# W_out products in merged runs, the last store in halves, and one 40-column product in the attention stage

## The chip, the cores and the metric

The kernel runs on one core of a Trainium2 chip. Its engines are TensorE (PE, with its weight loads shown apart as PEld), VectorE (DVE), ScalarE (ACT), GpSimd (POOL) and SyncE (SP, which here only issues DMAs). The metric is the device time of one launch in microseconds (us); lower is better.

## The reference

Three stages follow one another: a two-step attention over packed tokens, a mixture of experts with one expert for each token, and a dense layer pair with a sigmoid gate. Cut to what matters:

```
p_packed = sm_attn(p, k, v)                    # 8 batches, 8 heads, 576 tokens of 64; 32 packed tokens
x        = sm_attn(q, p_packed, p_packed)      # softmax attention, then tokens x 512
logits   = normed(x) @ normed(expert_emb).T / tau     # 8 experts
out[t]   = gate[t] * (relu(x[t] @ w1[e]) @ w2[e]),  e = argmax(logits[t])
h        = out @ w_in                          # 4608 x 512 by 512 x 2048
y        = (h * sigmoid(h)) @ w_out            # 2048 x 512
```

## The kernel before, in words

**Attention (`attention`, lines 1497 to 1890).** For each of 8 batches, `keys` makes the scores of the packed queries, `packs` the packed values and `queries` the second attention. Every operation is recorded with a cost, and `Sched.run` then makes one order for all engines: it takes the operation that can start first by these costs, with the table `TIMES` as priority. A changed cost or a changed buffer therefore moves work all over this stage. SP's loads keep the order in which they are recorded.

`packs` runs two times per batch (t = 0, 1). It transposes the packed values into PSUM, copies them to a tile `ppT` (a ring of two), and from `ppT` come three things: two POOL copies into `pt2` (line 1703), one POOL copy into `R.pp` (1709), and a small PE group `mp`: four products of 32 columns (values by values, line 1716) and four of 8 columns (values by expert embeddings `enT`, line 1719). DVE then takes `mp` into `ppf` (lines 1724, 1725), the operand of `queries`.

**Experts (from about 180 us) and the first dense layer (`group`, to about 850 us).** The change leaves both as they are. All matrix products are in split precision: an operand is a rounded high part (`hi`, a cast on ACT) and the rest (`lo`, a subtraction on DVE). The first dense layer writes its results as 2x2 blocks c11, c12, c21, c22 of a seven-product (Strassen-like) scheme into the DRAM tiles `c_d`.

**W_out (the end of `ffn`, from about 850 us).** There are 18 units `u` (each 256 rows of the output); a unit is seven products, in the order 1, 7, 6, 2, 5, 3, 4 (`order3`). Product i takes an operand of 128x1024: 1 and 6 take c11, 7 takes c21, 2 takes c12, 5 takes E1, 3 takes S4, 4 takes c22. `split(s)` makes its `hi` (ACT, line 1169) and `lo` (DVE) into one of four slots, two products ahead of use; the slots repeat with s mod 4. Besides, DVE makes the sums c11 = E1 - c11, S4 = c12 - c11 and, for the 14 units from u = 4 on, c21 = c11 - c21. For those units E1 is made by two DMAs into one tile: a plain load issued by SP (line 1186) and an adding one issued by POOL (line 1187) once the first has landed; the next unit's pair is started by `early_sums` when this unit's E1 has been split. `load_unit` loads the four blocks of the unit after the next.

From u = 2 on a product is "wide": eight matmuls of 512 columns with `hi` as weights (against high and low part of the output weights side by side, line 1202), then eight of 256 columns with `lo` (line 1200). Only the last unit's product 4 is narrow (256 columns throughout, lines 1204, 1205). A unit has four PSUM banks, and the units take two sets in turn: 1 and 2 add up in the first bank, 6 and 5 in the second, 7 and 4 in the third, 3 in the fourth. `drain` takes a bank into SBUF between them: P1 (after 1), U2 (after 6), V (after 5), and the two output tiles `outs[u]`; `write` stores these through SP (lines 1246, 1250). A bank's next product waits for the drain.

Of the kernel before, what the change touches and what calls it, by code (L numbers as in the profile page):

```python
# [871 lines left out]
def ffn(tc, st, sums, y_d, wf_d, t_d, c_d, u_d, out):  # L872
# [290 lines left out]
    def split(s):  # L1163
# [16 lines left out]
    def early_sums(u):  # L1180
# [3 lines left out]
        c11, c12, c21, c22 = raws[u % 2]  # L1184
# [3 lines left out]
        tt(DVE, c21, c11, c21, ALU.subtract)  # L1188

    def product(s, gs, start=True, stop=True):  # L1190
# [6 lines left out]
        for g, part in [(g, y) for y in (0, 1) for g in gs]:  # L1197
# [12 lines left out]
    def drain(s):  # L1210
# [16 lines left out]
        elif i == 6:  # L1227
            plus(U2, b, P1)
        elif i == 2:
            alone(outs[u][0][:, 0:256], a)  # L1230
        elif i == 5:
            plus(V, b, P1)
            plus(outs[u][1][:, 256:512], c, V)
# [3 lines left out]
        if i == 5 and not wide(u, 4):  # L1237
            plus(U2, c[1:], U2)
# [4 lines left out]
    def write(z, r, x, o):  # L1243
# [193 lines left out]
    for s in range(len(seq)):  # L1437
# [23 lines left out]
        if s == 4:  # L1461
            make(*more[4])

# [9 lines left out]
def attention(tc, sc, st, early, mid, R, first, ident, q, k, v, p, emb, tau, a2_d, scale, pairs):  # L1473
# [73 lines left out]
    enT = Part(1, [64, H, E])  # L1547

    def setup():
# [29 lines left out]
        op("DVE", 130, lambda: DVE.tensor_copy(out=enT.ap, in_=ep.ap), r=[ep], w=[enT])  # L1579
# [75 lines left out]
    def packs(b):  # L1655
        x2 = pt2[b % NB]
        for t in range(2):
# [39 lines left out]
            tT = T([128, 128], "ppT", 2)  # L1697
            op("PE", 109, lambda a=a, d=d: PE.transpose(out=a.ap, in_=d.ap.rearrange("p i d -> p (i d)"), identity=ident), r=[d], w=[a], hold=[tT])
            op("DVE", dve_c(128), lambda a=a, tT=tT: DVE.tensor_copy(out=tT.ap, in_=a.ap), r=[a], w=[tT])

            def f(tT=tT, t=t):
                for i in range(2):
                    POOL.tensor_copy(out=x2.ap[64 * i:64 * i + 64, 4 * t:4 * t + 4, 32 * i:32 * i + 32], in_=tT.ap[64 * i:64 * i + 64, :].rearrange("p (h j) -> p h j", h=4))
# [3 lines left out]
            def f(tT=tT, t=t):  # L1707
                h = slice(64 * t, 64 * t + 64)
                POOL.tensor_copy(out=R.pp[b][h, :, 32 * t:32 * t + 32], in_=tT.ap[h, :].rearrange("p (c j) -> p c j", c=4))
# [238 lines left out]
```

## Time and profile before

| | us |
|---|---|
| runs shown, median (lowest to highest) of 3 | 1216.39 (1213.45 to 1219.03) |
| the profiled execution's own time | 1214.78 |
| its span on the core | 1212.9 |
| PE busy | 1173.9 (97% of the span) |
| DVE busy | 876.9 (72%) |
| ACT busy | 526.4 (43%) |
| POOL busy | 146.9 (12%) |

Rows are read from this one profiled execution. A busy PE means that some matmul is in flight; since matmuls overlap, the distance from one start to the next, not the duration, is what a matmul costs. Times of day in the rows count from the span's start.

### The profile page before, as it was taken

How to read it: one execution, taken by the hardware profiler on the slowest of the kernel's cores; microseconds unless marked ns; L12 is line 12 of the kernel's file. 1: busy time of each engine (PE TensorE's matmuls, PEld its weight loads, DVE VectorE, ACT ScalarE, POOL GpSimd, SP SyncE). 2: the span in 40 equal slices, each digit the busy share in tenths (PEclk: the TensorE clock that was granted, in tenths of full speed). 3: DMA queues.
4: the chain of work that ended last, by engine and by line, in shares of the span. 5: the costliest groups of instructions: out<-in, count | busy, mean ns of one | idle time of the engine just before them, and what ended most of it. 6: DMA issues, size and time to landing. Idle time of an engine off the chain costs nothing.

```text
span 1212.9 us, 24417 instructions
## 1 busy us (share of the span) xinstructions
PE 1173.9 (97%) x9548; PEld 1034.1 (85%) x9549; DVE 876.9 (72%) x1560; ACT 526.4 (43%) x911; POOL 146.9 (12%) x259
## 2 busy tenths in 40 slices
PE   8788899999999999999999999999999999999998
PEld 7676679999989998978878878889998888888887
DVE  5475877886897883586765585634878888888886
ACT  4565652333343233464445354434643333333342
POOL 3222220221132432100000000002000000000000
PEclk9999999999999999999999999999999999999999
DMA  9979657569668965576876745788855657575652
GB/s 260 258 222 264 213 184 248 189 245 336 248 233 297 341 209 164 168 231 194 312 253 200 233 142 147 229 260 259 273 212 173 189 176 216 161 221 164 208 145 49
DMA packets 228313, 264.62 MB, mean 218 GB/s; under 512 B 32024, under 2 KB 181784, under 8 KB 227680
## 3 DMA queue, kind: packets, MB, share of 16 engines
q1 hardware_dynamic: 213192, 230.66, 59.2%
q0 software_dynamic: 8048, 27.53, 8.4%
q10 hardware_dynamic: 6952, 4.80, 1.3%
q8 instruction: 77, 1.26, 0.4%
q14 instruction: 44, 0.36, 0.1%
HBM read 175.26 MB, written 87.69 MB: 217 GB/s over the span
## 4 chain that ended last, share of the span: by engine, by line
PE 56%; DVE 3%; issue 1%; ACT 1%; DMA 0%; SPq 0%; DVEq 0%; ACTq 0%
PE p L1202 17%; PE p L1200 10%; PE p L906 8%; PE p L908 8%; PE p L907 8%; PE ps L620 2%; DVE x L899 1%; PE p L1205 1%; PE p L1204 1%; PE ps L541 1%; DVE raw L899 0%; DMA raw<-y_d 0%; DVE mh L899 0%; DMA c_d<-x 0%; DVE y L899 0%
## 5 line engine op out<-in xcount | busy, mean ns | idle before, releaser
L899 DVE TENSOR_TENSOR x<-p,x 128x512 f32<-128x512 f32 (+1 forms) x148 | 90.2, 619 | 58.8 <-PE p L908 52.8
L940 ACT ACTIVATE x<-x 128x512 f32<-128x512 f32 (+1 forms) x111 | 66.7, 603 | 137.5 <-DVE x L899 125.5
L620 PE MATMUL ps<-hkm,w2s 128*128 128x288 f32 x768 | 123.5, 296 | 0.0
L620 PEld LDWEIGHTS ps<-hkm,w2s 128*128 128x128 f32 x768 | 108.5, 188 | 5.9 <-DVE cu L678 1.7
L541 PE MATMUL ps<-at,mh 128*128 128x288 f32 x672 | 93.1, 297 | 4.2 <-PEq L735 2.1
L541 PEld LDWEIGHTS ps<-at,mh 128*128 128x128 f32 x672 | 90.5, 188 | 5.4 <-issue 3.5
L1202 PE MATMUL p<-x,x 128*128 128x512 f32 x332 | 90.4, 394 | 0.0
L620 PE MATMUL ps<-hvm,w2s 128*128 128x288 f32 x448 | 85.3, 295 | 0.0
L1202 PEld LDWEIGHTS p<-x,x 128*128 128x128 f32 x332 | 62.7, 189 | 10.8
L620 PEld LDWEIGHTS ps<-hvm,w2s 128*128 128x128 f32 x448 | 68.3, 188 | 0.1
L899 DVE TENSOR_TENSOR x<-p,y 128x512 f32<-128x512 f32 (+1 forms) x57 | 33.1, 581 | 42.8 <-PE p L908 39.1
L899 DVE TENSOR_TENSOR y<-p,y 128x256 f32<-128x256 f32 (+1 forms) x71 | 34.5, 485 | 35.4 <-PE p L1200 27.3
L1169 ACT CAST x<-rawe 128x1024 fp32r<-128x1024 f32 x35 | 36.4, 1051 | 49.5 <-DVE rawe L899 49.5
L620 PE MATMUL ps<-hqm,w2s 128*128 128x288 f32 x320 | 52.7, 294 | 0.0
L544 ACT ACTIVATE hkm<-ps 128x576 fp32r<-128x576 f32 x42 | 27.3, 652 | 55.7 <-PE ps L541 50.0
L630 ACT COPY yb<-ps 128x576 f32<-128x576 f32 x20 | 12.8, 642 | 88.3 <-PE ps L620 84.8
L1202 PE MATMUL p<-t,x 128*128 128x512 f32 x166 | 51.1, 389 | 0.0
L1187 POOL DMA_DIRECT2D x<-c_d x14 | 12.1, 865 | 319.8 <-DMA x<-c_d 223.1
L620 PEld LDWEIGHTS ps<-hqm,w2s 128*128 128x128 f32 x320 | 46.0, 188 | 0.0
L906 PE MATMUL p<-x,t 128*128 128x512 f32 x112 | 43.9, 392 | 1.5 <-DVE x L899 1.0
L591 DVE TENSOR_TENSOR w2s<-w2c,w2s 128x1024 fp32r<-128x1024 f32 x32 | 40.1, 1252 | 7.2 <-ACT w2s L588 7.2
L1222 ACT COPY raw<-p 128x256 f32<-128x256 f32 x18 | 6.7, 373 | 86.4 <-PE p L1200 86.4
(442 smaller groups left out, 3235.1 us busy)
## 6 DMA issues: line engine op xcount, KB each, us to landing
c_d<-x SPq DMA_DIRECT2D x136, 256.0 KB, 2.9
raww1c<-c_d SPq DMA_DIRECT2D x36, 512.0 KB, 6.1
rawe<-c_d SPq DMA_DIRECT2D x36, 512.0 KB, 5.0
w1c<-in_moe_w_dram SPq DMA_DIRECT2D x32, 512.0 KB, 10.4
w2c<-in_moe_w_dram SPq DMA_DIRECT2D x32, 512.0 KB, 4.0
y_d<-yb SPq DMA_DIRECT2D x36, 288.0 KB, 2.1
raw<-y_d SPq DMA_DIRECT2D x36, 256.0 KB, 4.8
x<-c_d SPq DMA_DIRECT2D x18, 512.0 KB, 3.9
```

Of the source, the lines that this page charges most:

```text
L541: PE.matmul(out=a[:, i, 0:H2], lhsT=mh[x][:, t, f], rhs=at[y][:, t, n], start=t == x == y == 0, stop=t == x == 1, skip_group_check=True)
L544: self.nc.scalar.activation(out=self.hT(0, m).rearrange("p (i n) -> p i n", i=2), in_=a[:, :, 0:S // 2], func=ACTF.Relu)
L591: DVE.tensor_tensor(out=l, in0=w2c[c % 2], in1=h.bitcast(F32), op=ALU.subtract)
L620: PE.matmul(out=a[:, i, 0:H2], lhsT=w[:, k, :], rhs=hT(z, k, n), start=w is h and k == z == 0, stop=w is l and k == 7, skip_group_check=True)
L899: eng.tensor_tensor(out=o, in0=x, in1=y, op=op)
L906: PE.matmul(out=o, lhsT=h, rhs=a[0][k][:, 0:n], start=start and k == 0, stop=False, skip_group_check=True)
L907: PE.matmul(out=o, lhsT=h, rhs=a[1][k][:, 0:n], start=False, stop=False, skip_group_check=True)
L908: PE.matmul(out=o, lhsT=l, rhs=a[0][k][:, 0:n], start=False, stop=k == 1, skip_group_check=True)
L940: ACT.activation(out=y, in_=x, func=ACTF.Silu)
L1169: ACT.copy(out=slots[s % R][0], in_=src)
L1200: PE.matmul(out=o, lhsT=l[:, g], rhs=x[:, 0:256], start=False, stop=stop and g == gs[-1], skip_group_check=True)
L1202: PE.matmul(out=bank, lhsT=h[:, g], rhs=x, start=first and g == gs[0], stop=False, skip_group_check=True)
```

## The change

In `ffn`, for u of 2 and more, a unit's products are emitted in three runs: (1, 7, 6), (2, 5) and (3, 4). A run first does the 512-column parts of its products one after another, then their 256-column parts. The drains, the splits and the loads are placed by hand between the 256-column parts. The sums S4 (16 units) and c21 (14 units) go from DVE to POOL. Product 7 is drained early, by an ACT copy and one DVE sum, and V is added later; DVE's count of 256-column drain operations in a unit stays 12. In the last unit the second output tile is stored in two column halves, the first when product 5 is drained, the second after product 4, one of its two DMAs on ACT's queue.

In `attention`, the embeddings stand beside the transposed values in one tile of 40 columns per head pair (`ppT`, now four fixed tiles), so that each group `mp` is four products of 40 columns.

```diff
-                tt(DVE, S4, c12, c11, ALU.subtract)
+                tt(POOL if u > 1 else DVE, S4, c12, c11, ALU.subtract)
...
+    def early_sums(u, loads=True):
+        if loads:
+            early_load(u)
+        if units[u][0] not in FIVE:
+            c11, c12, c21, c22 = raws[u % 2]
+            tt(DVE if loads else POOL, c21, c11, c21, ALU.subtract)
...
-        for g, part in [(g, y) for y in (0, 1) for g in gs]:
+        for g, part in [(g, y) for y in parts for g in gs]:
...
+        elif i == 7 and u > 1:
+            alone(outs[u][1][:, 256:512], c)
...
+                tt(DVE, outs[u][1][:, 256:512], outs[u][1][:, 256:512], V)
+                if u + 1 == len(units):
+                    write(z, r, 1, outs[u][1], slice(256, 512))
...
-            write(z, r, 1, outs[u][1])
+            write(z, r, 1, outs[u][1], slice(0, 256 if u + 1 == len(units) else 512))
...
-                SP.dma_start(out=out[(j + i) * S + 512:(j + i + 1) * S, :], in_=o[64 * i:64 * i + 64, :])
+                (ACT if i and n.stop == 256 else SP).dma_start(out=out[(j + i) * S + 512:(j + i + 1) * S, n], in_=o[64 * i:64 * i + 64, n])
...
+    for u in range(2, len(units)):
+        s = M + (u - 2) * len(order3)
+        for first, run in ((0, 3), (3, 2), (5, 2)):
+            for x in range(first, first + run):
+                product(s + x, range(G), parts=(0,))
+            for x in range(first, first + run):
+                i = order3[x]
+                product(s + x, range(G), parts=(1,))
+                if i not in (1, 7, 3):
+                    drain(s + x)
+                if i == 1:
+                    drain(s)
+                    hi(s + 4)
+                    lo(s + 4)
+                    if u + 1 < len(units):
+                        early_load(u + 1)
+                        early_sums(u + 1, False)
+                elif i == 6:
+                    drain(s + 1)
+                    hi(s + 5)
+                    lo(s + 3)
+                    lo(s + 5)
+                elif i == 2:
+                    hi(s + 6)
+                elif i == 5:
+                    hi(s + 7)
+                    lo(s + 6)
+                    if u + 2 < len(units):
+                        load_unit(u + 2)
+                    lo(s + 7)
+                    hi(s + 8)
+                elif i == 3:
+                    lo(s + 8)
+                    hi(s + 9)
+                    drain(s + x)
+                elif i == 4:
+                    lo(s + 9)
+                    hi(s + 10)
...
-            tT = T([128, 128], "ppT", 2)
+            tT = ppT[b % 2][t]
...
                 for c in range(4):
-                    h = slice(32 * c, 32 * c + 32)
-                    PE.matmul(out=m.ap[h, 0:32], lhsT=tT.ap[0:64, h], rhs=tT.ap[0:64, h], start=True, stop=True)
-                for c in range(4):
-                    h = slice(32 * c, 32 * c + 32)
-                    PE.matmul(out=m.ap[h, 32:32 + E], lhsT=tT.ap[0:64, h], rhs=enT.ap[:, 2 * c + t, :], start=True, stop=True)
-            op("PE", 200, f, r=[tT, enT], w=[m], after=o.users).mode = 3
+                    PE.matmul(out=m.ap[32 * c:32 * c + 32, :], lhsT=tT.ap[0:64, c, 0:NP], rhs=tT.ap[0:64, c, :], start=True, stop=True)
+            op("PE", 130, f, r=[tT], w=[m], after=o.users).mode = 3
```

**Attention, PE.** The order differs from the first `mp` groups of batch 0 on. Before (pptp: transposed packed values; mp: the small group; ktp, krp: transposed keys; s2p, s1p: scores):

```order
L1698 MATMUL pptp<-ident,ppd 128x128
L1716 MATMUL mp<-ppT 32x32 x4
L1719 MATMUL mp<-e_148,ppT 32x8 x4
L1716 MATMUL mp<-ppT 32x32 x4
L1719 MATMUL mp<-e_148,ppT 32x8 x4
L1624 MATMUL ktp<-ident,km 128x128 x8
L1611 MATMUL krp<-ident,kr 128x64 x4
L1753 MATMUL s2p<-e_148,qT 64x2x32 x16
L1638 MATMUL s1p<-kT,pT 32x256 x8
```

Here the two groups, 16 products in all, stood right behind the transposes.

After, at the same place:

```order
L1765 MATMUL pptp<-ident,ppd 128x128
L1691 MATMUL ktp<-ident,km 128x128 x4
L1678 MATMUL krp<-ident,kr 128x64 x4
L1691 MATMUL ktp<-ident,km 128x128 x4
L1816 MATMUL s2p<-e_148,qT 64x2x32 x16
L1705 MATMUL s1p<-kT,pT 32x256 x8
L1710 MATMUL s1p<-kTr,e_148 32x32 x8
L1782 MATMUL mp<-e_148 32x40 x8
```

The groups are eight products now and have moved behind key transposes and both kinds of scores; from here on the whole stage's PE order is another one.

**W_out, PE, the first wide unit (u = 2).** p6, p0, p7 are PSUM banks, e1, x2, x5 slots, the other names output weights. Before, product 1 and the start of product 7:

```order
L1202 MATMUL p6_7413<-mh1_143,e1_3513 128x512
L1202 MATMUL p6_7413<-x0_7399,e1_3513 128x512 x4
L1202 MATMUL p6_7413<-mh1_143,e1_3513 128x512
L1202 MATMUL p6_7413<-t0_7818,e1_3513 128x512
L1202 MATMUL p6_7413<-t1_7894,e1_3513 128x512
L1200 MATMUL p6_7413<-mh1_143,e1_3513 128x256
L1200 MATMUL p6_7413<-x0_7399,e1_3513 128x256 x4
L1200 MATMUL p6_7413<-mh1_143,e1_3513 128x256
L1200 MATMUL p6_7413<-t0_7818,e1_3513 128x256
L1200 MATMUL p6_7413<-t1_7894,e1_3513 128x256
L1202 MATMUL p0_7407<-mh1_143,x2_7402 128x512
```

Each product is eight of 512 columns, then eight of 256.

After, from the end of product 7's 512-column part:

```order
L1207 MATMUL p0_7330<-t1_7817,x2_7325 128x512
L1207 MATMUL p7_7337<-mh0_142,x5_9858 128x512
L1207 MATMUL p7_7337<-x0_7322,x5_9858 128x512 x4
L1207 MATMUL p7_7337<-at1_140,x5_9858 128x512
L1207 MATMUL p7_7337<-t0_7741,x5_9858 128x512
L1207 MATMUL p7_7337<-t1_7817,x5_9858 128x512
L1205 MATMUL p6_7336<-mh1_143,e1_3436 128x256
L1205 MATMUL p6_7336<-x0_7322,e1_3436 128x256 x4
L1205 MATMUL p6_7336<-mh1_143,e1_3436 128x256
L1205 MATMUL p6_7336<-t0_7741,e1_3436 128x256
L1205 MATMUL p6_7336<-t1_7817,e1_3436 128x256
L1205 MATMUL p0_7330<-mh1_143,e1_3436 128x256
```

The 256-column parts of 1 and 7 now follow the 512-column part of 6: a unit passes from 256 to 512 columns three times, not seven times.

**W_out, POOL, the whole stage before** (t1: output weights, x4: E1):

```order
L1333 DMA t1_7894<-wf_d_67 128x256
L1334 DMA t1_7894<-wf_d_67 128x2x256
L1335 DMA t1_7894<-u_d_94 128x4x256
L1187 DMA x4_7403<-c_d22_81 128x1024 x4
L1187 DMA x4_7403<-c_d02_71 128x1024 x4
L1187 DMA x4_7403<-c_d32_86 128x1024 x4
L1187 DMA x4_7403<-c_d42_91 128x1024 x2
```

POOL did nothing there but issue the 14 adding DMAs.

After, the first units (x6: S4; raww1c and rawe0: the units' blocks in turn):

```order
L899 TENSOR_TENSOR x6_9859<-raww1c_9915 128x1024
L899 TENSOR_TENSOR x6_9859<-rawe0_10095 128x1024
L1193 DMA x4_7326<-c_d22_81 128x1024
L899 TENSOR_TENSOR raww1c_9915<-raww1c_9915 128x1024
L899 TENSOR_TENSOR x6_9859<-raww1c_9915 128x1024
L1193 DMA x4_7326<-c_d22_81 128x1024
L899 TENSOR_TENSOR rawe0_10095<-rawe0_10095 128x1024
L899 TENSOR_TENSOR x6_9859<-rawe0_10095 128x1024
```

From u = 4 on each unit's adding DMA is followed in POOL's queue by c21 and then S4.

**The end, SP's queue before** (x4: the last unit's E1, raw: output tiles):

```order
L1246 DMA out_0_dram<-raw_12618 128x512
L1186 DMA x4_7403<-c_d43_92 128x1024
L1250 DMA out_0_dram<-raw_12770 64x512 x2
L1250 DMA out_0_dram<-raw_12771 64x512 x2
L1250 DMA out_0_dram<-raw_12921 64x512 x2
L1250 DMA out_0_dram<-raw_12922 64x512 x2
```

The last unit stored its first output tile (12921), then its second.

After:

```order
L1258 DMA out_0_dram<-raw_12571 128x512
L1192 DMA x4_7326<-c_d43_92 128x1024
L1262 DMA out_0_dram<-raw_12724 64x512 x2
L1262 DMA out_0_dram<-raw_12725 64x512 x2
L1262 DMA out_0_dram<-raw_12877 64x256 x2
L1262 DMA out_0_dram<-raw_12876 64x512 x2
L1262 DMA out_0_dram<-raw_12877 64x256
```

The second tile's right half (12877) now goes ahead of the first tile (12876), and one DMA of the left half comes last; the other stands at the end of ACT's queue.

## Rows read from the trace of the kernel before

**Rows 1.** Stretches: length, busy us (count) of PE, PEld, DVE, ACT, POOL; clock; DMA.

```profile
0.00:180.00 180.00, 156.87 (x3278) 124.73 (x3286) 116.50 (x381) 104.89 (x246) 45.46 (x120) 0.99 0.82 236
895.30:1205.40 310.10, 310.10 (x1778) 272.91 (x1778) 255.51 (x346) 117.87 (x142) 12.11 (x14) 1.00 0.57 171
```

**Rows 2.** Timeline, PE, first dense layer: start us, duration us, line, tiles, count.

```profile
780.23 0.40 PE L906 MATMUL p<-x,t 128*128 128x512 f32 x1
...
782.07 0.39 PE L908 MATMUL p<-x,t 128*128 128x512 f32 x1
...
783.88 0.39 PE L907 MATMUL p<-x,t 128*128 128x512 f32 x1
```

**Rows 3.** Chain that ended last, W_out: start us, us that it adds, line.

```profile
874.41 0.96 PE p L1200 x8
...
895.53 1.84 PE p L1202 x8
897.37 0.95 PE p L1200 x8
```

**Rows 4.** Timeline, PE, two small groups of the attention stage.

```profile
155.45 0.27 PE L1716 MATMUL mp<-ppT 64*32 64x32 f32 x8
155.53 0.22 PE L1719 MATMUL mp<-e,ppT 64*32 64x8 f32 x8
155.60 0.24 PE L1716 MATMUL mp<-ppT 64*32 64x32 f32 x8
```

**Rows 5.** Waits of PE, 0 to 180 us: total us, times, longest.

```profile
PE ppp L1690 <- issue: 4.1, 2, 2.2
PE s2p L1753 <- issue: 3.7, 2, 1.9
```

**Rows 6.** Stretches of the attention stage, columns as in group 1.

```profile
50.00:54.00 4.00, 1.84 (x65) 1.27 (x53) 1.59 (x4) 0.63 (x1) 0.00 (x0) 1.00 0.61 129
54.00:58.00 4.00, 3.90 (x32) 3.01 (x32) 1.89 (x6) 2.01 (x4) 2.92 (x8) 0.60 0.77 237
```

**Rows 7.** Timeline, ACT, W_out: after product 1, with what ended the wait.

```profile
1152.55 0.37 ACT L1222 COPY y<-p 128x256 f32<-128x256 f32 x1 [1.22 <-PE p L1200]
1152.82 1.06 ACT L1169 CAST x<-rawe 128x1024 fp32r<-128x1024 f32 x1
```

**Rows 8.** Timeline, DVE, W_out: two drain sums, a sum, a split.

```profile
1158.14 0.88 DVE L899 TENSOR_TENSOR y<-p,y 128x256 f32<-128x256 f32 x2 [1.81 <-PE p L1200]
1158.94 1.22 DVE L899 TENSOR_TENSOR raww1c<-raww1c 128x1024 f32<-128x1024 f32 x1
1160.07 1.22 DVE L899 TENSOR_TENSOR e<-x,e 128x1024 fp32r<-128x1024 f32 x1
```

**Rows 9.** Timeline, SP's and POOL's queues, W_out: the two DMAs of one E1.

```profile
1156.35 0.33 SPq L1186 DMA_DIRECT2D x<-c_d  x1
...
1160.76 0.86 POOL L1187 DMA_DIRECT2D x<-c_d  x1 [18.63 <-DMA x<-c_d]
```

**Rows 10.** DMA issues from 950 us on: count, KB each, median us to landing.

```profile
x<-c_d POOLq DMA_DIRECT2D x12, 512.0 KB, 6.2
```

**Rows 11.** Groups by line and form, POOL: busy us, mean ns, idle us.

```profile
L1768 POOL TENSOR_TENSOR a2s<-e,sm 128x512 f32<-128x512 f32 x16 | 16.7, 1048 | 45.7 <-DVE lg_all L1803 13.9 <-ACT qT L1740 10.6 <-DVE sq L1802 9.7
...
L1843 POOL TENSOR_TENSOR a2s<-e,sm 128x256 f32<-128x256 f32 x4 | 2.5, 618 | 11.7 <-ACT qT L1740 7.1 <-ACT kT L1629 2.8 <-DVE sq L1802 1.4
```

**Rows 12.** Timeline, POOL, experts stage: sums of two SBUF operands.

```profile
235.85 0.74 POOL L696 TENSOR_TENSOR y<-co 128x256 f32<-128x256 f32 x1
```

**Rows 13.** Line 316, DVE: ns min/median/max, first and last start.

```profile
L316 DVE TENSOR_TENSOR x<-x,x x16: 411/416/957, 504.2 to 643.8; 128x256 fp32r<-128x256 f32 x16
```

**Rows 14.** Timeline, the last matmuls and the last DVE operation.

```profile
1208.06 0.40 PE L1200 MATMUL p<-t,x 128*128 128x256 f32 x2
1208.50 0.42 DVE L899 TENSOR_TENSOR raw<-p,y 128x256 f32<-128x256 f32 x1 [1.99 <-PE p L1200]
```

**Rows 15.** Line 1250, SP's issues of stores of 64 rows: ns min/median/max.

```profile
L1250 SPq DMA_DIRECT2D out_dram<-raw x8: 466/560/589, 1187.0 to 1209.5; - x8
```

More of the change, by code (lines that the diff above doesn't have):

```diff
@@ L1183, in early_sums @@
             return
-        c11, c12, c21, c22 = raws[u % 2]
         z, r = units[u]
@@ L1187, in early_sums, with product @@
         POOL.dma_start(out=E1, in_=c_d[z][2][:, r].rearrange("p g n -> p (g n)"), accum_op=ALU.add)
-        tt(DVE, c21, c11, c21, ALU.subtract)
-    def product(s, gs, start=True, stop=True):
+    def product(s, gs, start=True, stop=True, parts=(0, 1)):
         u, i = seq[s]
@@ L1230, in drain @@
             alone(outs[u][0][:, 0:256], a)
+        elif i == 7 and u > 1:
+            alone(outs[u][1][:, 256:512], c)
+            if not wide(u, 4):
+                plus(U2, c[1:], U2)
         elif i == 5:
             plus(V, b, P1)
-            plus(outs[u][1][:, 256:512], c, V)
+            if u > 1:
+                tt(DVE, outs[u][1][:, 256:512], outs[u][1][:, 256:512], V)
+                if u + 1 == len(units):
+                    write(z, r, 1, outs[u][1], slice(256, 512))
+            else:
+                plus(outs[u][1][:, 256:512], c, V)
         if i == (3 if u else 5):
@@ L1236, in drain, with write @@
             write(z, r, 0, outs[u][0])
-        if i == 5 and not wide(u, 4):
-            plus(U2, c[1:], U2)
         if i == 4:
             plus(outs[u][1][:, 0:256], c[:1 + wide(u, 4)], U2)
-            write(z, r, 1, outs[u][1])
-    def write(z, r, x, o):
+            write(z, r, 1, outs[u][1], slice(0, 256 if u + 1 == len(units) else 512))
+    def write(z, r, x, o, n=slice(0, 512)):
         if z < NP2:
@@ L1436, in ffn @@
     PLAN = {0: (4,), 1: (), 2: (), 3: (5,), 4: ()}
-    for s in range(len(seq)):
+    M = 2 * len(order3)
+    for s in range(M):
         n, (u, i) = s, seq[s]
@@ L1462, in ffn, with hi, lo @@
             make(*more[4])
+    los = {}
+    def hi(s):
+        if s < len(seq):
+            h, los[s] = split(s)
+            h()
+    def lo(s):
+        if s in los:
+            los.pop(s)()
+    hi(M + 2)
+    lo(M + 2)
+    hi(M + 3)
+    for u in range(2, len(units)):
[36 more added lines that the diff above has]
+                    hi(s + 10)
 def act_c(n):
@@ L1546, in attention @@
     pt2 = [Part(1, [128, H, 64]) for i in range(NB)]
-    enT = Part(1, [64, H, E])
+    ppT = [[Part(1, [128, 4, NP + E]) for t in range(2)] for i in range(2)]
     def setup():
@@ L1578, in setup @@
         op("PE", 400, tr, r=[esq], w=[ep])
-        op("DVE", 130, lambda: DVE.tensor_copy(out=enT.ap, in_=ep.ap), r=[ep], w=[enT])
+        for i in range(4):
+            o = ppT[i // 2][i % 2]
+            op("DVE", 110, lambda i=i, o=o: DVE.tensor_copy(out=o.ap[0:64, :, NP:], in_=ep.ap[:, i % 2::2, :]), r=[ep], wp=[o])
         for i in range(NB):
@@ L1708, in f @@
                 h = slice(64 * t, 64 * t + 64)
-                POOL.tensor_copy(out=R.pp[b][h, :, 32 * t:32 * t + 32], in_=tT.ap[h, :].rearrange("p (c j) -> p c j", c=4))
+                POOL.tensor_copy(out=R.pp[b][h, :, 32 * t:32 * t + 32], in_=tT.ap[h, :, 0:NP])
             op("POOL", 300, f, r=[tT], wp=[R.ppF[b]])
```

8 lines of the change are left out of this document (4 added, 4 removed).

## Prediction

> **What bounds the kernel now.** I read the stretches first [rows 1]. In W_out PE is busy for all of 310.1 us at granted clock 1.00, while DVE is busy for 255.5 and ACT for 117.9: there only fewer or closer matmuls can save time, and every wait that the change adds to PE costs in full. In the attention stage PE is busy for 156.9 of 180 us, at a mean clock of 0.99; the other 23 us are holes. The waits of PE name the largest of them "issue", two of some 2 us each at `ppp` and at `s2p` [rows 5]: they come out of the order on the engines, not out of the amount of PE work. The experts and the first dense layer stay as they are.
>
> The profiled execution took 1214.78 us, 1.6 below the median 1216.39. I sum against the profiled time and add 1.6 at the end.
>
> **W_out, matmuls.** The changes take no matmul away, so a gain can only come from the passage between widths. A product is 1.84 us for eight of 512 columns and 0.95 for eight of 256 [rows 3], 2.79 in all. What a passage costs I read where two wide parts follow each other: in the first dense layer the first eight of 512 columns take 782.07 - 780.23 = 1.84 us, the next eight 1.81 [rows 2]. So entering 512 columns costs 0.03. Entering 256 gains 0.01 back: eight take 0.96 where 256 columns went before, 0.95 behind 512 [rows 3]. A passage there and back costs 0.02. There were 16 x 7 - 1 = 111 wide products with one passage each; now there are 16 x 3 = 48. Gain: 63 x 0.02 = **1.3 us**. By the bare step of 0.03 it would be 1.9.
>
> The Trainium skill ("TensorE: Matmul & The Clock Gate", Back-to-back issue gap) gives N/2.4 + 2.5 ns for a matmul alone, an estimate of 2.60 us for a product, 0.19 less than the trace's. Were the passages to blame for that, the merge could win much more; the rows say that they are not, since a long run of 512 columns keeps 1.81/8 = 0.226 us each [rows 2]. That result has its rival below.
>
> **W_out, do the waits stay covered?** Count from the start of a unit, which is now 19.48 us long (7 x 2.79 less some 0.05 for four passages). Run (1, 7, 6) has its last 512 columns at 5.5 and ends at 8.3; run (2, 5) lasts to 13.9; run (3, 4) to 19.5. Three chains could come late.
>
> First, bank 2. Product 6 ends at 8.3 and product 2 covers 1.84 before 5 writes the same bank at 10.2. Drains P1 and U2 must be through by then. Product 1's low part follows at 5.5 and has left PE at about 6.6; ACT copies it, 0.27 until its next operation [rows 7]; DVE's queue then holds a split, 1.13 until the next start, and two drain sums, 0.88 [rows 8], and ACT's cast before the split takes 1.06 [rows 7]. 6.6 + 0.27 + 1.06 + 1.13 + 0.88 = 9.94, against 10.2. The margin is about 0.2; each tenth that is missing would cost 16 x 0.1 = 1.6 us. I take 0.
>
> Second, E1. Product 5's operand is split by 6.6 + 0.27 + 1.06 + 1.22 = 9.2, then the next unit's E1 can be loaded. The row before shows 4.4 us from the plain load's issue to the adding one on POOL [1156.35 to 1160.76, rows 9], which holds POOL for 0.86 [rows 9] and lands 6.2 after its issue [rows 10]: 9.2 + 4.4 + 6.2 = 19.8. c11 on DVE (1.22) and its cast (1.06) end at 22.1; product 7 of the next unit wants it at 19.5 + 2 x 1.84 = 23.1 or a little before, as product 6's operand. About 1 us is left: 0.
>
> Third, POOL. It had no arithmetic in W_out, 12.1 us in all for its DMAs [rows 1]; now it has 16 sums S4 and 14 sums c21 of 128x1024. No row shows that form. From 618 ns for 256 columns and 1048 for 512 [rows 11], 1.68 ns a further column, comes 1.05 + 512 x 0.00168 = 1.9 us; sums of two SBUF operands take 0.74 for 256 [rows 12] where the others take 0.62, so 1.9 x 0.74/0.62 = 2.3; four times 0.74 is the upper end, 2.94. I take 2.3, as both operands lie in SBUF. DVE is not held by this through data but by a shared resource: the same DVE sum of two SBUF operands takes 416 ns at the median and up to 957 [rows 13], in the stage where POOL runs such sums [rows 12].
>
> The Trainium skill ("SBUF — State Buffer", Who interferes with whom) states that a VectorE instruction with two SBUF inputs and a GpSimd instruction that reads SBUF exclude each other, the one that comes second waiting for the whole of the first. The 957 agrees; no row shows it for 1024 columns. By the rule c21 always holds DVE where the two meet; by the median of [rows 13] alone it would hardly ever; the first rival below says what that is worth.
>
> I count with the hold from the rows. POOL is free of its DMA at 9.2 + 4.4 + 0.86 = 14.5 and runs c21 until 14.5 + p. DVE meanwhile has some 0.3 of an output sum and the 1.22 split of product 4 to do [rows 8], and product 4's low part is wanted at 18.4. So PE waits only for p above 18.4 - 14.5 - 0.3 - 1.22 = 2.4 us. At 2.3 that is 0; at 2.94 it is 14 x 0.54 = 7.6. DVE itself has room: 255.5 us in 15.9 units of 19.55 us are 16.1 each [rows 1], less two sums of 1.22 that leave it is 13.7, and with a hold of up to 2.3 for each POOL sum still under 19.5. S4 falls beside drains that read PSUM. I take **0, bounds 0 to +7.6**. A gain from the relieved DVE is excluded, because PE did not wait for it [rows 1].
>
> **The attention stage.** A group `mp` was two halves, one 0.08 us behind the other, and the next group came 0.15 after the first [rows 4]. Four products of 40 columns should cost about what four of 32 did, 0.08 to 0.09. 16 groups x 0.063 = **1.0 us** less PE work; DVE's three more small copies in the setup lie beside loads. But PE has holes here, and the lower cost reorders all engines, the groups themselves moving behind key transposes and both kinds of scores. A hole is worth about 2 us [rows 5]; and after a stretch with PE busy for 1.84 of 4 us the next four run at granted clock 0.60, between the levels 1.2 and 2.4 GHz, with PE 3.90 busy [rows 6]: 4 x 0.4 = 1.6 us of work lost. So one hole more or less is 2 to 3.6 us. Fixed tiles instead of a ring of two let `ppT` be written earlier, which speaks for a gain; the groups' later place, for a loss of what `queries` waits for. I see no reason for a sign: **0, bounds -4 to +4**, about one such hole either way.
>
> **The end.** Before, the last matmuls start at 1208.06, the last drain ends at 1208.50 + 0.42 = 1208.92 [rows 14], and two SP issues follow, 0.56 each at the median [rows 15], before the data is on its way. Now the right half goes out early. But product 3's low part ends 0.95 before the last matmul does, and its two drain sums take 0.88 [rows 8], so SP begins the first tile's two issues, 1.1 us by [rows 15], only at the last matmul. Product 4's half, ready 0.4 later, stands behind them with one issue; ACT makes the other beside it. SP's last issue begins some 1.15 us after the last matmul, where it was 1.0 before; undivided it would be 1.7. I take **+0.1**.
>
> **Sum.** -1.3 - 1.0 + 0.1 + 0 + 0 = -2.2; 1214.8 - 2.2 = 1212.6, and 1.6 to the median: **1214.2 us**. A measurement of this kernel can tell about 0.5%, 6.1 us, from no change (1210.3 to 1222.5), so that this forecast is "the same".
>
> **The rivals.**
> *POOL's sums hold DVE until PE waits.* Mechanism: c21 starts on POOL at 14.5 in each of 14 units, keeps DVE from the split of product 4, and PE stands before product 4's low part; it decides from p = 2.4 us on. For it: no idle time in PE's 310 us to take it up, and the 957 ns [rows 13]. Against it: p is 2.3 by the slope, and DVE has 5 us of room in a unit. At p = 2.94 the time is 1214.2 + 7.6 = 1221.8; if POOL besides waits for a DVE sum of 1.22 in progress, half of it on average, p counts as 3.5 and it is 14 x 1.1 = 15 more, 1229.
> *The new attention order is worse.* One or two holes more, with a clock dip each: +2 to +7, 1216 to 1221.
> *The new attention order is better.* One or two holes of [rows 5] go: -2 to -7, 1207 to 1212.
> *The merge wins more than the passages.* A matmul of 512 columns takes 0.226 us in a run and one of 256 0.119 (0.95/8), so 256 columns cost 0.107 and 0.012 is fixed in each. If long runs took that away, a product would save 16 x 0.012 = 0.19 us and 111 of them 21: 1195. For it: nothing else here could show so much. Against it: the eight that follow eight of their own width still take 1.81 [rows 2]. The Trainium skill's formula, named above, leads to the same 0.19.
> *The change does not do what it says.* DVE's or ACT's drains come late at bank 2, so that PE passes from run to run with a wait: 0.2 us for each unit eats the 1.3 and more, +3.2, 1217.
>
> **How the numbers follow.** Forecast, nothing waits: 0.44. POOL's hold 0.20, of which 0.09 beyond 1222.5. Worse order 0.12, of which 0.03 beyond 1222.5. Better order 0.16, of which 0.11 below 1210.3. Late drains 0.05. Merge wins more 0.03, below 1210.3. Faster: 0.11 + 0.03, and 0.02 of the forecast's own where part of two gains meets, 0.16. Slower: 0.09 + 0.03 = 0.12. Same: 0.72. The range may leave out 0.2: it goes from 1208, reached by a better order of two holes, to 1222, POOL's hold at p = 2.94, with about 0.10 left out on either side.
>
> **What would show it.** In the profile after: units of 19.5 us by PE's distances in W_out, and no wait of PE there for DVE or POOL (steps one and three); a sum of 128x1024 on POOL near 2.3 us, and DVE splits that take longer than 1.22 beside it but no PE wait behind them; groups `mp` 0.085 apart; the attention stage ending within 4 us of where it did, its holes and low clock stretches counted; the last issue about 1.1 us after the last matmul. The forecast is wrong if the POOL sum is longer than 2.4 us and PE waits for slot 4's split, or if the attention stage moves by over 4 us.

## The result and the profile after

| | before | after |
|---|---|---|
| median of 21 runs each, us (lowest to highest) | 1215.39 (1210.07 to 1220.88) | 1220.86 (1215.62 to 1227.57) |
| ratio to before, 95% interval | | 1.0053 [1.0039, 1.0067] |
| profiled execution: its own time, us | 1214.78 | 1224.45 |
| first matmul of the first dense layer, us | 498.73 | 505.58 |
| first wide matmul of W_out, us | 895.36 | 902.67 |
| end of the last matmul, us | 1208.46 | 1218.32 |
| end of the span, us | 1212.92 | 1222.71 |

The change makes the kernel about 6.4 us slower (1215.39 x 0.0053). The forecast was 2.2 us faster; 1220.86 lies inside the range, near its upper end, and the sign is wrong. That it lies inside is luck: the upper end was there for POOL's hold in W_out, and most of the loss comes from the attention stage. The profiled execution of after is 3.6 us above its median, so the profiles differ by more (9.8 us) than the runs do. The marks say where: +6.9 us by the end of attention and experts, +0.5 in the dense layer that the change leaves alone, +2.5 in W_out, and -0.1 at the end.

The two stretches that answer to [rows 1] (columns as there):

```profile
0.00:180.00 180.00, 156.28 (x3066) 122.81 (x3067) 111.37 (x368) 99.75 (x234) 45.27 (x120) 0.96 0.80 223
902.60:1212.00 309.40, 308.39 (x1758) 268.46 (x1758) 256.14 (x311) 122.75 (x158) 84.93 (x44) 1.00 0.58 172
```

In the first 180 us PE is as busy as before, but it has got through less: 3066 matmuls, and the 212 that are missing against 3278 are more than the 128 that the change removes in the whole stage (64 products, each of which the profile records as two matmuls). The granted clock is 0.96 where it was 0.99. In W_out PE is 1.0 us short of fully busy, and POOL, which did almost nothing there, works for 85 us.

PE's waits in the attention stage, answering to [rows 5]:

```profile
PE xp L1853 <- issue: 2.4, 1, 2.4
PE ppp L1757 <- issue: 2.0, 2, 1.2
PE s2p L1891 <- DVE sm L1827: 1.6, 1, 1.6
PE mp L1782 <- issue: 1.5, 1, 1.5
PE e1rp L1738 <- ACT a2f L1842: 1.5, 1, 1.5
...
PE xp L1853 <- DVE lg_all L1866: 1.3, 1, 1.3
PE a0p L541 <- DVE mh L510: 1.2, 1, 1.2
```

Before, the three largest rows of this list were "issue", and of the waits for another engine that near the start of the stage was the largest:

```profile
PE xp L1860 <- issue: 2.4, 1, 2.4
PE e1p L1665 <- ACT e L1652: 1.5, 2, 1.1
```

Now four single waits for DVE and ACT of 1.2 to 1.6 us stand among the largest that were not there before: they come out of the new order. The worst place is 124 to 144 us. Its rows of PE, and its stretches (columns as in [rows 1]):

```profile
125.82 0.47 PE L1853 MATMUL xp<-e,a2f 64*64 64x72 f32 x15 [1.28 <-DVE lg_all L1866]
128.74 0.52 PE L1853 MATMUL xp<-e,a2f 64*64 64x72 f32 x17 [2.44 <-issue]
...
139.17 0.98 PE L1891 MATMUL s2p<-pp,qT 128*64 128x64 f32 x16 [1.58 <-DVE sm L1827]
```

```profile
124.00:128.00 4.00, 1.02 (x47) 0.74 (x42) 1.96 (x6) 1.62 (x6) 1.05 (x1) 1.00 1.12 325
128.00:132.00 4.00, 3.26 (x62) 1.90 (x65) 1.61 (x7) 1.24 (x5) 0.00 (x0) 0.64 1.03 408
...
136.00:140.00 4.00, 2.42 (x75) 2.15 (x66) 3.79 (x14) 2.14 (x7) 2.16 (x5) 0.92 0.21 69
140.00:144.00 4.00, 4.00 (x27) 3.62 (x28) 3.16 (x13) 2.24 (x5) 0.62 (x1) 0.65 0.16 54
```

A wait for the logits (`lg_all`) and a hole of 2.44 us leave PE busy for 1.02 of 4 us, and a wait for the softmax sums (`sm`) leaves it busy for 2.42 of 4; in the stretch behind each the granted clock is 0.64 and 0.65, between the two levels. That is the pair of costs that the prediction had read from [rows 6], only several times over.

W_out, one quiet unit in the chain that ended last (start us, us that it adds, line; L1207 is 512 columns, L1205 is 256):

```profile
1060.46 5.48 PE p L1207 x24
1065.94 2.87 PE p L1205 x24
1068.82 3.72 PE p L1207 x16
1072.54 1.91 PE p L1205 x16
1074.45 3.65 PE p L1207 x16
1078.10 1.91 PE p L1205 x16
```

The sum is 19.54 us; before, seven times 1.84 + 0.95 [rows 3] took 19.55 from unit to unit by the starts. The merged runs save next to nothing, though they are as written. The run (3, 4) needs 3.65 for sixteen of 512 columns, the run (2, 5) needs 3.72: product 5 is slow to start, as its rows show:

```profile
912.39 0.62 PE L1207 MATMUL p<-t,x 128*128 128x512 f32 x2
912.85 0.43 PE L1207 MATMUL p<-mh,e 128*128 128x512 f32 x1
913.11 1.08 PE L1207 MATMUL p<-x,e 128*128 128x512 f32 x4
```

From the start of product 5 to its second matmul are 0.26 us in place of 0.227, and behind that the eight run through the slow start of a run again (starts 0.23 to 0.24 apart). And some units are not quiet. Over 15 units the starts lie 293.30 us apart before and 295.84 after; six of the 15 units are 0.16 to 0.9 longer than 19.55.

### The profile page after: what moved, and what is told of

The parts are those of the page before. It is cut to its first block, busy times and chain, and to the rows that moved or that the text cites. A ratio compares the mean times of both kernels' runs of the same rounds, so it can differ in the third digit from the quotient of the medians.

```text
span 1222.7 us, 24239 instructions
## 1 busy us (share of the span) xinstructions
PE 1182.6 (97%) x9420; PEld 1037.7 (85%) x9421; DVE 879.9 (72%) x1533; ACT 532.0 (44%) x927; POOL 220.3 (18%) x289
## 4 chain that ended last, share of the span: by engine, by line
PE 28%; issue 28%; DMA 3%; DVE 1%; ACT 1%; POOL 0%; SPq 0%; ACTq 0%; POOLq 0%; DVEq 0%
PE p L1207 14%; PE p L1205 8%; PE ps L620 2%; DMA x<-c_d 2%; PE ps L541 1%; PE p L1210 1%; PE p L1209 1%; DMA x<-wf_d 1%; DVE x L899 0%; DMA rawe<-c_d 0%; ACT x L1169 0%; DVE x L316 0%; PE p L906 0%; PE p L908 0%; PE p L907 0%
## 5 line engine op out<-in xcount | busy, mean ns | idle before, releaser
L541 PE MATMUL ps<-at,mh 128*128 128x288 f32 x672 | 95.7, 302 | 3.1 <-PEq L735 2.1
L541 PEld LDWEIGHTS ps<-at,mh 128*128 128x128 f32 x672 | 93.1, 193 | 4.1 <-issue 3.4
L1207 PE MATMUL p<-x,x 128*128 128x512 f32 x332 | 89.8, 392 | 0.0
L1207 PEld LDWEIGHTS p<-x,x 128*128 128x128 f32 x332 | 62.5, 188 | 11.5
L1207 PE MATMUL p<-t,x 128*128 128x512 f32 x166 | 51.3, 390 | 0.0
L1169 ACT CAST x<-raww1c 128x1024 fp32r<-128x1024 f32 x32 | 33.2, 1050 | 28.7 <-DVE raww1c L899 16.9
L899 DVE TENSOR_TENSOR x<-x,x 128x1024 fp32r<-128x1024 f32 (+2 forms) x45 | 40.6, 902 | 7.0 <-ACT x L1169 4.2
```

The lines of the kernel that those rows point to most:

```text
L541: PE.matmul(out=a[:, i, 0:H2], lhsT=mh[x][:, t, f], rhs=at[y][:, t, n], start=t == x == y == 0, stop=t == x == 1, skip_group_check=True)
L899: eng.tensor_tensor(out=o, in0=x, in1=y, op=op)
L1169: ACT.copy(out=slots[s % R][0], in_=src)
L1207: PE.matmul(out=bank, lhsT=h[:, g], rhs=x, start=first and g == gs[0], stop=False, skip_group_check=True)
```

## The experiments

A ratio is to the kernel before, with its 95% interval; 0.001 is 1.2 us. "End" is the start of the first dense layer in the one profiled execution, the end of what the attention order can touch.

**e1, e2: each half of the change alone.** The diff of e1 is the diff's part from line 1544 on, that of e2 the part ahead of it.

> The attention part of the change alone, W_out as before. Theory (the new attention order makes the loss): as in the trace of the changed kernel the stage ends 5 us later and the first dense layer starts about 7 us later, so 4 to 7 us slower than before; W_out units stay at 19.55 us. Rival (the late attention of that one profile was chance, W_out makes the loss): within 1 us of before, and in this profile the first dense layer starts within 2 us of 498.7.

> The W_out part of the change alone, attention as before. Theory: W_out loses 1 to 2.5 us in a few waits of PE for c11 and for product 4's low part, since quiet units are 19.55 us as before; 1 to 3 us slower, with the first dense layer at 498.7 within 2 us. Rival (W_out makes the whole loss): 5 to 6 us slower.

Measured: attention alone 1.0040 [1.0020, 1.0060], its end 507.22; W_out alone 1.0016 [0.9990, 1.0042], its end 497.28. The late attention stage is no chance of one profile: it is there again, with the same waits (`s2p` for `sm` 1.7, `xp` for `lg_all` 1.3). W_out's loss can't be told from zero by its time, but by its trace: 15 units take 296.76 us for 293.30, in the same two kinds of wait as after. So attention makes most of the loss, and the rival that W_out makes all of it falls.

**e3, e4: the products without the order, the order without the products.** In e3 the planner is told what it was told before and only the emitted instructions are new; every engine's order is before's. In e4 the order is the change's, and a group is made of eight products again.

```diff
+w = ppT[b % 2][t]
...
-op("DVE", dve_c(128), lambda a=a, tT=tT: DVE.tensor_copy(out=tT.ap, in_=a.ap), r=[a], w=[tT])
+op("DVE", dve_c(128), lambda a=a, w=w: DVE.tensor_copy(out=w.ap[:, :, 0:NP], in_=a.ap.rearrange("p (c j) -> p c j", c=4)), r=[a], w=[tT])
...
+PE.matmul(out=m.ap[32 * c:32 * c + 32, :], lhsT=w.ap[0:64, c, 0:NP], rhs=w.ap[0:64, c, :], start=True, stop=True)
 op("PE", 200, f, r=[tT, enT], w=[m], after=o.users).mode = 3
```

> Attention with the products of 40 columns and the fixed tiles, but every engine's order as before; W_out as before. If the order is what costs, this has only the smaller PE work: groups mp 0.085 us apart, 0 to 1.3 us faster. If the products or the strided copies cost themselves, it is slower by a good part of 5 us.

> Attention in the changed kernel's order with fixed tiles, but with the eight products of 32 and 8 columns for each mp group; W_out as before. If the order is what costs: 5 to 8 us slower, about 1 more than the attention part alone. If the products cost, within 1 us of before.

Measured: products alone 0.9947 [0.9929, 0.9965], 6.4 us faster than before, its end 493.95; order alone 1.0048 [1.0027, 1.0068], its end 505.86. By e4 the order costs 5.8 us, and by e3 the products gain. That they gain 6 and not 1 was in no expectation. A pair of groups takes 0.278 us to the next start where it took 0.366, which, with less for single groups, makes some 0.5 us for all 16. The rest had to be elsewhere on PE, with the same order. Comparing the two traces step by step, e3 pulls ahead where before had a hole named "issue" and e3 has none: at 53.01 before stood still for 2.16 us in the middle of its products `ppp`, and e3 ran through.

```profile
50.44 0.66 PE L1694 MATMUL ppp<-vm,e1T 128*32 128x64 f32 x32
51.02 0.32 PE L1694 MATMUL ppp<-vr,e1Tr 64*32 64x64 f32 x8
51.27 0.46 PE L1615 MATMUL krp<-ident,kr 64*128 64x64 f32 x4
```

(e3, timeline of PE.) That led to a count. If all of PE's instructions in the trace (matmuls, weight loads and the semaphore instructions between them) are numbered from 0, the first matmul or weight load behind every such hole of over 0.5 us in the attention stage of before has a number 193 + 256 n: n = 4, 5, 6, 8, 15, 16 and 18 for the seven holes. The page lists a DMA queue of the kind "instruction":

```profile
q8 instruction: 77, 1.26, 0.4%
```

(before, its DMA queues: packets, MB, share.) Packets of 16 KB; 77 times 256 is 19,712, about PE's stream, of which the trace has 19,262 instructions, 19,097 of them matmuls and weight loads. The packets pair off with the holes: before instruction 193 + 256 n PE waits for the n-th packet of this queue and goes on 1.15 to 1.55 us after that packet has ended, in each of the seven. So a hole named "issue" here is PE without code. The change takes away 128 matmuls and 128 weight loads, as many as one block holds. The Trainium skill ("Runtime: NRT & Kernel Launch", Instruction fetch mechanics) has the blocks of 256 instructions, and says that crossing one is mostly hidden; the trace agrees with the 256, but seven of some 25 crossings in this stage together cost 12.0 us before.

**e5, e6, e7: shift the code, not the work.** Two of the 18 warm-up products ahead of the stage are replaced by 40 tiny ones, 152 PE instructions more, in before, after and e3.

```diff
-        for i in range(18):
+        for i in range(16):
             PE.matmul(out=warm.ap[:, i % 4, :], lhsT=ident, rhs=ident, start=True, stop=True)
+        for i in range(40):
+            c = i % 4
+            PE.matmul(out=warm.ap[32 * c:32 * c + 32, 0, 0:32], lhsT=ident[0:64, 0:32], rhs=ident[0:64, 0:32], start=True, stop=True)
```

> The kernel before with 152 more PE instructions in the warm-up ahead of the stage (two of its 18 products replaced by 40 tiny ones), nothing else. Theory (the holes named issue are waits for PE's code, which comes in blocks of 256 instructions at positions 193 + 256 n): all such holes now stand at 193 + 256 n again, that is before other matmuls than at ppp 53.0, xp 66.6 and s2p 110.0 and 127.8; their sum of 12.0 us changes by 2 to 5 us either way and the time with it, for the same work. Rival (they stand before those matmuls because of the work there): the same holes before the same matmuls, time within 1.5 us of before.

> The changed kernel with the same 152 instructions in the warm-up. Theory (code waits and the clock dips behind them are part of its 7 us in the attention stage, waits of the new order the other part): holes at 193 + 256 n elsewhere, time 3 us or more away from the changed kernel's in one of the two directions, while the waits on xp for ACT and DVE (about 13 us of other idle time to the stage's end) stay. Rival (the order's own waits are all): within 1.5 us of the changed kernel.

> The 40-column products in the old order, with the 152 instructions in the warm-up. If most of the 6 us that they gained were a matter of where the code blocks fall, this moves by 2 to 5 us again, either way; if the gain is the 64 products that are gone, it stays within 1.5 us of 0.9947 of before.

Rows of PE that wait for "issue", before and then e5:

```profile
39.23 0.43 PE L1690 MATMUL ppp<-vm,e1T 128*32 128x64 f32 x16 [1.90 <-issue]
45.12 0.45 PE L1828 MATMUL s2p<-pp,qT 128*64 128x64 f32 x8 [1.23 <-issue]
53.01 0.32 PE L1690 MATMUL ppp<-vm,e1T 128*32 128x64 f32 x8 [2.16 <-issue]
66.62 0.47 PE L1860 MATMUL xp<-e,a2f 64*64 64x72 f32 x13 [2.44 <-issue]
```

```profile
22.84 0.20 PE L1719 MATMUL mp<-e,ppT 64*32 64x8 f32 x2 [2.22 <-issue]
...
58.30 0.67 PE L1638 MATMUL s1p<-kT,pT 64*32 64x256 f32 x16 [0.85 <-issue]
66.00 0.69 PE L1753 MATMUL s2p<-e,qT 128*64 128x64 f32 x7 [3.09 <-issue]
93.01 0.66 PE L1638 MATMUL s1p<-kT,pT 64*32 64x256 f32 x13 [0.54 <-issue]
```

The holes stand before other matmuls, again at 193 + 256 n. In all 14 profiles every hole of over 0.5 us named "issue" in the first 200 us has such a number, and ends 1.15 to 1.8 us after the n-th packet. (Shorter ones need not: 0.50 us at 33.03 in e5 is named "issue" and has another number.) That the holes are waits for code is thereby shown. The price was expected wrongly: e5 is 1.0001 [0.9983, 1.0018] of before, e6 1.0040 [1.0018, 1.0063] against 1.0053 of after, and only e7 moved, from 0.9947 to 0.9979 [0.9959, 0.9998]. Which matmul a hole meets does not decide the time; its sum differs between executions of one order too (the holes named "issue" at these numbers make 9.1 to 12.0 us in the five profiles with before's attention). What I keep of the products' gain is therefore both values, -6.4 us in e3 and -2.5 in e7.

**e8: c21 back on DVE**, W_out alone.

```diff
-            tt(DVE if loads else POOL, c21, c11, c21, ALU.subtract)
+            tt(DVE, c21, c11, c21, ALU.subtract)
...
-                        early_sums(u + 1, False)
...
                     lo(s + 6)
+                    if u + 1 < len(units):
+                        early_sums(u + 1, False)
```

> The W_out part alone, with c21 back on DVE (behind product 6's split, S4 still on POOL). If POOL's hold on DVE makes the wait of 0.9 us before product 4's low part, that wait is gone; the waits of 0.3 to 0.6 us before product 6's high part stay if E1's late landing makes them, and go if the hold did. 0.5 to 2.5 us less than the W_out part alone.

First what the two kinds of wait look like in the profile of after. One is POOL's hold (timelines of DVE, POOL and PE):

```profile
1134.07 3.10 DVE L899 TENSOR_TENSOR raw<-raw,x 128x256 f32<-128x256 f32 x1
1137.09 1.21 DVE L899 TENSOR_TENSOR x<-rawe,x 128x1024 fp32r<-128x1024 f32 x1
...
1134.18 2.70 POOL L899 TENSOR_TENSOR raww1c<-raww1c 128x1024 f32<-128x1024 f32 x1
...
1138.36 0.39 PE L1205 MATMUL p<-mh,x 128*128 128x256 f32 x1 [0.65 <-DVE x L899]
1138.58 0.64 PE L1205 MATMUL p<-x,x 128*128 128x256 f32 x4
```

A sum of 256 columns on DVE, both operands in SBUF, takes 3.10 us because c21 on POOL runs through it; the split of product 4 starts at 1137.09, and PE stands before its low part. The other is E1 (timelines of POOL, DVE, ACT and PE):

```profile
1014.70 0.88 POOL L1193 DMA_DIRECT2D x<-c_d  x1 [8.81 <-DMA x<-c_d]
...
1022.27 1.22 DVE L899 TENSOR_TENSOR raww1c<-x,raww1c 128x1024 f32<-128x1024 f32 x1 [0.58 <-DMA x<-c_d]
...
1023.61 1.05 ACT L1169 CAST e<-raww1c 128x1024 fp32r<-128x1024 f32 x1 [4.52 <-DVE raww1c L899]
...
1024.71 0.50 PE L1207 MATMUL p<-mh,e 128*128 128x512 f32 x1 [0.31 <-ACT e L1169]
1025.05 0.62 PE L1207 MATMUL p<-x,e 128*128 128x512 f32 x2
```

The adding DMA is issued 13.95 us into the unit, c11 waits for its landing until 21.5, and PE for the cast. Measured in e8: 1.0007 [0.9984, 1.0029]; the times can't tell it from e2, the traces can. The sum on DVE is back at its length,

```profile
1027.85 0.42 DVE L899 TENSOR_TENSOR raw<-raw,x 128x256 f32<-128x256 f32 x1
```

no wait before product 4's low part is left, and five waits for product 6's high part remain. 15 units take 295.11 us, 1.65 less than in e2 and 1.81 more than before. So the hold makes one kind of wait; the other, by the trace, is E1, started at 9.2 us of a unit where it was at 6.8. A run with E1 started earlier is not among these.

**e11: the second bank free earlier**, a single execution, on top of e8.

```diff
                 if i == 1:
                     drain(s)
                     hi(s + 4)
-                    lo(s + 4)
-                    if u + 1 < len(units):
-                        early_load(u + 1)
                 elif i == 6:
+                    lo(s + 4)
+                    if u + 1 < len(units):
+                        early_load(u + 1)
                     drain(s + 1)
```

> The W_out part with c21 on DVE and product 5's split moved behind the drain of product 6, so that the second bank is free earlier and E1 later. If the missing gain of the merge goes into a wait for that bank at the start of product 5 (first distance 0.267 us in place of 0.226, then a new start of the 512-column run), units 2 and 3, which load no E1 by pairs, are 19.48 us long where they were 19.54; the later units wait for E1 by about 1 us more each, 10 us in all. If the merge itself gives nothing, units 2 and 3 stay at 19.54.

```profile
926.05 0.62 PE L1207 MATMUL p<-t,x 128*128 128x512 f32 x2
926.50 0.39 PE L1207 MATMUL p<-mh,x 128*128 128x512 f32 x1
926.73 1.07 PE L1207 MATMUL p<-x,x 128*128 128x512 f32 x4
```

(e11, the start of product 5.) The 0.26 is 0.23 now and the sixteen run through, so the wait for the bank was real. But the gain does not come out: units 2 and 3 are 19.66 and 19.67 long, not 19.48, since the split that was moved back now comes late for the low part of its product (0.2 us in each), and the later units wait for E1, 19.9 to 24.7 long. Its time was 1234.14. The bank, the split and E1 stand in one queue on DVE; that a free bank gives 19.48 is not shown.

**e9, e10: other orders.** e9 is e1 with the cost of `mp` left at 200; e10 is e3 with the cost at 130. Each has one more order.

> The attention part alone with the planner's cost of a group mp left at 200; the fixed tiles ppT and the four small copies of the setup remain, and with them an order that is again another one than before's and than the change's. If the lower cost is what makes the order bad: within 2 us of the products in the old order (0.9947 of before). If any new order loses against the one that the table of priorities belongs to: 3 to 7 us slower than that, more other idle time than the 10 to 15 us of the old order, and more clock loss than 1.7 to 4.4 us.

> The 40-column products with the planner told what it was told before (ring of two, one copy in the setup), but with the cost of mp at 130. Also another order, closer to before's. By 'any new order loses': 3 us or more slower than the products in the old order; by 'the fixed tiles in the plan make it': within 2 us of it.

Measured: 1.0056 [1.0034, 1.0078] and 1.0036 [1.0016, 1.0056], their ends at 507.10 and 507.37, 13 us behind e3 with the same products. Their largest waits are again others, for the keys' load in e9 and for the largest of `lg_all` in e10:

```profile
PE ktp L1626 <- DMA km<-in_k_dram: 3.4, 4, 1.4
```

```profile
PE a0p L541 <- DVE mx L378: 3.1, 2, 1.8
```

So neither the lower cost nor the fixed tiles are the one culprit: the planner, told of either alone, makes an order that loses. All three new orders were made with the table `TIMES` that stood with the old one; what a table fitted to the new costs would give was not tried.

**e12: the whole change in the old order.**

> The whole change (40-column products, fixed tiles, W_out in runs, sums on POOL, store in halves) with the attention stage's order kept as before. By the sum of the parts (products in the old order -6, W_out +1 to +2): 4 to 5 us faster than before, 10 us under the changed kernel; if W_out's part of the loss is larger together with the rest, no faster than before.

Measured: 0.9983 [0.9965, 1.0001], end 495.32. The same products, W_out and stores as in the changed kernel, 7.0 in 1000 or 8.5 us less than it. The gain over before is 2.1 us where the parts promised 4 to 5, within what the intervals leave open. W_out's 15 units took 295.17 us, 1.9 more than before.

The account of PE's time up to the first dense layer, counted from the profiles (means where there are several; us). "End" is the start of that layer. The next three columns are of the first 200 us, where the attention stage ends: "code" is all idle time of PE directly ahead of instructions 193 + 256 n, "other idle" all the rest in which no matmul was in flight, and "clock" is busy time times what the granted clock lacks to 1.00 in stretches of 2 us. What is left of the end without the three is 471 to 474 in every row.

| order, products | profiles | end | code | other idle | clock |
|---|---|---|---|---|---|
| before's, old | before, e2, e5, e8, e11 | 497.4 | 11.0 | 10.5 | 2.9 |
| before's, new | e3, e7, e12 | 494.5 | 7.0 | 11.3 | 3.2 |
| the change's, new | after, e1, e6 | 504.3 | 9.1 | 16.5 | 5.8 |
| the change's, old | e4 | 505.9 | 9.0 | 18.0 | 7.5 |
| another, new | e9 | 507.1 | 4.3 | 20.8 | 8.5 |
| another, new | e10 | 507.4 | 6.3 | 21.9 | 4.8 |

From the second row to the third, the order costs 9.8 us: 5.3 of waits, 2.6 of clock and 2.1 of code, with 0.2 less in the rest. In the two columns that matter the ranges of the single profiles do not meet: other idle 9.8 to 11.8 in before's order and 15.5 to 18.0 in the change's, clock 1.7 to 4.4 and 5.1 to 7.5. The code column swings between profiles of one order and the same products (7.1 to 12.0 in the third row), so its 2.1 is not shown to belong to the order.

## Why the prediction was wrong, step by step

**The attention order: the step that failed.** "I see no reason for a sign: 0, bounds -4 to +4, about one such hole either way." It was +9.8 us in the profiles of the same products, 8.5 in the times of e12 and after; the four pairs of times with the same products on both sides (before and e4, e7 and e6, e12 and after, e3 and e1) give 5.8 to 11.3. The prediction's own sign of being wrong, an attention stage moved by over 4 us, is there. The mechanism was named among the rivals ("one or two holes more, with a clock dip each: +2 to +7"), with a chance of 0.12. Two things were wrong in it. There are more than two places, three at 125, 139 and 156 us alone. And the sign was hardly open: the three other orders that ran (the change's, e9's, e10's) all lose, by 8.5 to 13 us against e12 and e3, which have the old order and the same products, and by about 7 us and more against e7. What the list of waits before [rows 5] said, and I did not draw from it, is that the old order waits for other engines in short pieces only; its largest holes were all "issue". That such an order has more to lose than to gain is an argument that fits the three, not a thing shown. Why the planner's other orders are worse than its model takes them to be, the cause behind the waits, stays open.

**The holes named "issue".** "They come out of the order on the engines": wrong. They are waits for code (e5), and so could not be priced as gains or losses of an order. The reading also left out the largest single one, 2.4 us at `xp`.

**The 40-column products: right sign, too small.** -1.0 was forecast for PE's work; the groups' own time fell by 0.5. e3 and e7 gained 6.4 and 2.5 us. Of the mean difference of the ends, 2.8 us, the account finds 4.0 in the code column, with one block of code less, and 1.0 lost in the other two. The term that was missing is thus the wait for code. Why 128 matmuls less take so much of it away is not shown: one block is one crossing of some 25, and in the change's order the column is the same for the new products (9.1) and the old (9.0).

**W_out's merge: the passage's price was right, the gain was taken back.** Runs of 24 and 16 save about 0.08 us in a unit as forecast; the bank of products 6 and 5, to which I gave a margin of 0.1 to 0.2 us, had none, and product 5's late start takes 0.07 back. In the profile of after (unit from 1060.30) the two drain sums end 10.0 us into the unit, where the prediction had 9.94 and product 5 is due at 10.2:

```profile
1069.43 0.88 DVE L899 TENSOR_TENSOR y<-p,y 128x256 f32<-128x256 f32 x2
```

Product 5's first matmul starts at 1070.49, 0.2 us behind the sums, and holds the next back by 0.27 us; in e11, with the bank free earlier, it does not. What was left out is thus the way from DVE's end to PE, some 0.2 us as an estimate from these rows, for which I had counted nothing. A unit is 19.54 for 19.55, and of the 1.3 us some 0.1 is left.

**POOL's sums: right in size, nearly right in effect.** The forecast was 2.3 us each, with a wait of PE from 2.4 on:

```profile
L899 POOL TENSOR_TENSOR x<-rawe 128x1024 f32<-128x1024 f32 x8 | 19.3, 2414 | 53.2 <-issue 35.6 <-DVE rawe L899 17.6
...
L899 POOL TENSOR_TENSOR raww1c<-raww1c 128x1024 f32<-128x1024 f32 x7 | 18.9, 2698 | 0.0
```

(after, groups on POOL by form; in c21 the first 0.27 us lie beside the end of the DMA ahead of it.) S4 is 2.41, c21 2.70. (The prediction's upper end, four times 0.74, is 2.96 and not 2.94.) The POOL sum of [rows 12] is one of the experts stage; what stands beside the 957 of [rows 13], in the dense layer, are four other sums on POOL (line 309, 502.10 to 505.74). The hold on DVE came in each of the 14 units with a c21 on POOL: a sum of 0.42 us took 2.24 in the mean there (1.98 to 3.10), but only one unit passed it on to PE as a long wait. In that one DVE's sum ends 0.3 us behind POOL's (1134.07 + 3.10 and 1134.18 + 2.70 in the rows under e8). The Trainium skill's rule ("SBUF — State Buffer", Who interferes with whom) is thereby seen for a 1024-column operation: a DVE operation with two SBUF inputs waits for the whole of POOL's.

**E1: the slack was not there.** "About 1 us is left: 0." The adding DMA is issued at 13.5 to 14.6 us of a unit in the profile of after, where 13.6 was forecast; but the landing is late by up to 1.3 us against the median of 6.2, and c11 stands behind other splits on DVE, so that the 1.0 us is used up in four units out of 14 there, and in six, five and two in e2, e8 and e12. Together with the hold W_out lost 2.5 us in the profile of after and 1.8 to 3.5 in e2, e8 and e12, where 1.3 gained was forecast.

**The end: right.** SP's three issues run from 1218.31 for 1.96 us, ACT's beside them:

```profile
1218.31 1.96 SPq L1262 DMA_DIRECT2D out_dram<-raw  x3
...
1218.81 0.55 ACTq L1262 DMA_DIRECT2D out_dram<-raw  x1
```

The last issue begins 1.21 us after the last matmul's end (forecast 1.15), and from that end to the span's end are 4.39 us for 4.46: -0.1 where +0.1 was taken.

**The sum.** W_out +2.5, attention order +9.8, products -2.8, the first dense layer +0.5 and the end -0.1 make +9.9 in the profiles, where the two profiled spans differ by 9.8; in the runs it is +6.4. The best of all kernels is e3, the products alone in the old order, 0.9947 of before and 12.9 us under the changed kernel.

## What to carry to other kernels

Where a planner orders the work, a cheaper operation is two changes, and the new order is the larger one: make the operation cheap first while the planner is told the old costs, and measure the orders apart from it. Before taking a change of order for nothing, look at what the old order waits for; here three of three new orders lost against one whose waits for other engines were all short. In a hand-made schedule, a margin of a tenth of a microsecond counts as none, and work moved to POOL stops DVE's sums of two SBUF operands for its whole length.

## What the runs showed of the hardware

PE's code comes in packets of 16 KB for 256 instructions; where a packet lands late PE stops in the middle of a group, for up to 3.7 us (e4), at instructions 193 + 256 n of all 14 profiles, and goes on 1.15 to 1.8 us after the packet's end. This happened in the attention stage, where 256 instructions last some 6 us and the DMA engines are busy with loads (DMA column 0.80 to 0.85 over 180 us); in W_out, where they last over 20 us, PE has no idle time at all in before [rows 1]. That the loads delay the packets was only argued.

A wait costs more than itself: after one the first matmul of 512 columns holds the next back by 0.34 us in place of 0.227 (1024.71 to 1025.05 in the rows under e8), one of 256 columns by 0.22 in place of 0.12 (1138.36 to 1138.58), about 0.1 us more each time.
